# Batch 0's second halves behind all its first halves, four half transposes and two query pairs moved to DMA, and fewer bytes of loads in flight

## The chip, the cores and the metric

The kernel runs on one core of a Trainium2 chip. The metric is the device time of one execution in microseconds; the lower, the better. The core has five engines with queues of their own: TensorE (PE), which multiplies matrices; VectorE (DVE) and ScalarE (ACT), which copy and combine; GpSimd (POOL), which adds a little arithmetic and issues the loads from memory; and SyncE (SP), which issues the other transfers. The transfers themselves run on 16 shared DMA engines.

## The reference

The program is an attention with sorted blocks, followed by a bilinear feed-forward network. Four batches of eight heads, 768 positions and head width 64:

```python
for _ in range(5):                              # Sinkhorn steps on an 8x8 matrix per head
    P = np.exp(P - np.max(P, axis=-1, keepdims=True))
    P = P / (np.sum(P, axis=-1, keepdims=True) + 1e-09)
    P = P / (np.sum(P, axis=-2, keepdims=True) + 1e-09)
k_sorted = einsum('bhij,bhjcd->bhicd', P, k_blocks)      # mixes the 8 blocks of 96 rows
v_sorted = einsum('bhij,bhjcd->bhicd', P, v_blocks)
attn = softmax(scale * q_block @ k_sorted_block.T)       # within each block of 96
x = (attn @ v_sorted_block), heads side by side          # 3072 tokens x 512
out = ((x @ w_a) * (x @ w_b)) @ w_out                    # 512 -> 1536 -> 512
```

## The kernel before

**Staging.** The four batches go one after the other through two parts. The attention part works on pairs of heads (four pairs, `p` = 0 to 3, in a batch), so that two heads of 64 fill 128 partitions. It brings q into transposed form (`qT`), mixes k and v with the spread Sinkhorn matrix (`s_all`), forms scores, exponentials and the weighted sum of v, divides, and writes the result `xp` (96 rows of a block, by block, by head). `xp` is then transposed into `xT`, the tokens of a batch along the free dimension. The feed-forward part multiplies `xT` with `w_a` and `w_b`, multiplies the two results, and multiplies that with `w_out`. Batch 0 does this plainly (L836 for the first two products); batches 1 to 3 use sums of blocks in Strassen's manner for the first two products (L930), and all batches are plain at the last (L987).

**Halves.** In batch 0 each pair is cut in two halves of four blocks (`h` = 0, 1), because the plain products need only one half of the tokens at a time: `t` = 0 needs the first halves of all four pairs, `t` = 1 the second. For a half, `q_part` makes 12 transposes on PE (L555) and one copy to `qT`. `mix_half` makes 12 products for k and 12 for v (L582), each with a copy to `kT` or `vT`. `v_part` makes four transposes of `vT` on PE (L641) and a copy to `vs`. `so_part` makes eight score products (L660), an exponential on ACT (L665), eight products with `vs` (L675), a reciprocal (L681) and the division (L686), which writes `xp`. `x_part` transposes `xp` with four products on PE (L694) and copies the result to `xT`. The first pieces of the second half of a pair wait for the division of the first half of the same pair (`st["gate", p]`, L1171).

**Later batches.** `attention` handles a whole pair at once. Its q comes either by 12 PE transposes of 128 columns and a copy (`q_part`), or, where `QDMA(b, p)` holds (L262: batch 3), by `q_wide`, two loads on POOL in pieces of 64 elements, and one transposing transfer issued on SP (L707). In the second case the score products read `qT` with a stride. Their x always goes by one transposing transfer for a pair (L702). For most pairs v goes through memory and back (L628 out, L632 back), issued on SP.

**Loads.** `load` (L378) issues the loads from memory on POOL, one after the other. For each of the first 24 loads (q, k, v of batch 0 and the parts of `w_a` and `w_b`) it counts bytes backwards through the loads already issued; where the sum passes a limit (L383), the new load waits for that earlier load to have landed. Each load also waits for the seventh before it. The sum of bytes is that of the 4-byte source.

**Order.** All work is declared as pieces with dependencies, buffers and possible engines (`Plan.add`). The order in which they are issued, and the engine of those with a choice, come from the constant `ORDER`, two characters for each piece; the pieces of an engine run in that order. Into planned gaps of PE early in the kernel `_fill` puts wide products on a constant tile that nobody reads (L1222, called filler below). So a change in `ORDER` can move any piece.

Of the kernel before, what the change touches and what calls it, by code (L numbers as in the profile page):

```python
# [16 lines left out]
def _ap(t: bass.AP, extra_offset, pattern):  # L17
    return bass.AP(tensor=t.tensor, offset=t.offset + extra_offset,
                   ap=[list(p) for p in pattern])
# [17 lines left out]
class Plan:  # L37
# [192 lines left out]

RATE = 365e3
ORDER = (
    b"%z1C$e###%#'#)#+#/#-#1#5$g$i#7#;$k$m#A$o#=$q$s#G#3$u$w#C#M$y%^${#I$}#9#S%`%#%%#Y%'#O#?%)%+"
    b"#`#E%-%/#U#f%1%~%3#[#K%5#l&$%7%9#b#r%;#Q%=#W%?#x%A#h%C&@%E#n#^%G&B%I%K#t%M#d#~%O%Q%S#j$(#z"
    b"%U$.&_#p%W&a%Y$4%b%f#v%d$:%[$$&&%h&H)/&(%j&K%n%l&D&*#|%p&G&2$*&L&-&c$@&4$0%r&O&.)+$6%t&e&P"
    b"&1&g$<$&%v&R&o$B$,&j')&q$2'%$F',&T$8''&k&V'-$L$>&X&m&6&}$H)-'0&Z'#'f&8%x&^'^'h&:'b%|'j$D'a"
    b"&<'d$R$N&s'm'C&>&u'?-j'E&w'n'A'G(($J'p'J($$T'O(+$X'K(&'1'N'Q&y-r'|&|(,'3$P(#*0(/$Z*<$_*@-l"
    b"*>$V$a*2*D*B(>*8*4*F(D$]'S(@*6(J-_*H(P(F*:*T(V$c*J(L-Z(](B*V-c*P(c(R'U*L-e*](i(H*m'W(X-f*N"
    b"(N*X(_*R(T*o(o(e(0-i*u*a(u(Z-](k*Z(2({-a(a,8)%*_(q(4,:*c-v(g(6'Y(w*i(8*e(m+f'](}-p*g+i(s(:"
    b")''5*k(<*q(y)1+n'7*s'9)3)7+q)#'r)=*w';+r'=))-n-1+t't+j'v,4+l)9'x,<,7-t'z+v,>,]-3--)5,`+x,D"  # L240
    b")C,@-0,F-x*})?,C*y+z*{)I);+|+~+))O+%,H)E++)U,J,L,N)[)K+1+#)b)A+-,P+')Q)h,$)G+/,&)n)W+A+3)M"
    b")t,()^+C,*)S)z,e,,+I+5)d,g)Y*$+9)j+7,i)`**.Z+=)p,k,R.^+;)f,T+Y,V)v)l.c+?+M)|)r+[.e+O+b*&.g"
    b"+E)x,m+U/1*,.i+G/3)~,a+K,o-5,c*(+^-7+Q*..k,{-9,q,}+S.m+`,s+W-;._,.,00.+d.a/Y0*00,X/].y,2.o"
    b"0-.{,u.P,w.q-=,y,Z-?-#-A-%/^-'-C.(1E-)/`/5-+-K/7/--M.*/0/9.s.,/b.u/A.w../;-z/C/d/f.0/=/K-O"
    b"/M.}/h-Q-|/#/?.R/%-~02.T-E.$04.<-G-I06/j.&-S.V0>.>080@/E.A/O/l-U.2/G/Q.X/I.B/S-W/x0H0:/z/n"
    b".F.D/p0<0J1H/r/|/t1r/~/v.H1t.41I1v0$.J1L1z.6.L1x1M1|0B25.81~1O0D.N2$0F1U2&1Q.:1W2*2(1[1S26"
    b"202,1^221l1Y2.1`1b282:1h0L2<1j1d1n0N2>0P2B1f0V2D0X0]2@2_0c2H0_2a1q2F2Y2J2g0e0i2N0Z2c2i0o2L"
    b"2e0u0a2m2T0k2[2P2o2V0{2k0q2R2q1%0g4P0w2s4T2]2y3'0m4V2{3#2u3)0s3+4R2}2w3/1+3-4X313K0}0y4Z33"
    b"5#3M3%351'3S114]3F371-3O5%173U3;1#391=3Y3Q3A1)3=3[3C3G3W3?4e4_3j3^1/4g3`5O133z3I6L3f3h3l19"
    b"4a5Q4F151?1;3b6$4c/'0&3d4o6&3|3o5W4q/)5'5Y4H0(5)5S1A4#5[4<4J5|/+5U4L5^5d5~5+5f6(4$5-4(6*4N"  # L250
    b"5/5`4&6,4i/U4*514k574m4,5n5b4>0R594s6.4A425p/W4u534w4B0T646044664.5h55475r3p6N4D485j5t6S5l"
    b"625v6{405;6Q6}3r4:5=7#5?3t7'7%3v687)6V6T7+6:6X7>7-3x6<6_7/6Z6a73716e6]7?79756g7;6u6c776i6k"
    b"7A7C6q6>7E6s6w6m7G6@6o7K7I6y6B7M7h6D7O7c7j7Q6F7p7S7l7r7W7U7v7n7d7^7Y7x7`8*7t7[7z7|5A7f8&80"
    b"5C8(8,7~82848$5E88868.8T8:5G8<8O8V8>5I8]8@8X8_8D8B8c8Z8P8J8F8e8L8s8a8H8y8i8R8v9O8k9;4y5K8m"
    b"8x4{5M8g9'5x8o9Y4}8q6H5z8{9)8}9E6J9,9#9[9-919%9^9`9/9b9d939f9G969Q9I9l979T9h9n:u9U9j9=99:w"
    b"9r:'9K9?9p9W9t:y9A:}9x9M9v;#:{:(9z9~;'9C;79|;%;):$:*:,;-;+:.:0;:;3:4:2;/:6;5:J:8;1::;<;=:<"
    b";A;?:@:>;C:L;E:F:B;[:H;G;I:D;K:O:P;M:T:R;Q;O:V;^:X;W;S;Y:Z:o:];U:_;a;b:a;f;d:e:c;h:q;j:k:g"
    b":m;l<$;n:i;p:t<4;r;v<';t<H;|;~;x<R;z<)<J<T<L<6<W<><N<8<:<P<]<X<<<@<_<Z<B<*<b<D<c<,<F<.<0<e"
    b"<2"
)  # L260
STRASSEN_OUT = ()
QDMA = lambda b, p: b >= 3  # L262
VDMA = lambda b, p: 4 * b + p >= 6


@with_exitstack
def kernel(
# [11 lines left out]
    nc = tc.nc  # L279
    P = 128  # L280
    B, H, S, D = q.shape
# [96 lines left out]
    def load(fn, nbytes, deps=(), get=(), rank=0.0, many=0.0, spare=0.4):  # L378

        ds, way, behind = [d for d in deps if d is not None], nbytes, None  # L380
        for k in reversed(range(len(ld_n))):
            way += ld_n[k][1]
            if way > 2.8e6 and len(ld_n) < 24 and behind is None:  # L383
                behind = ld_i[k]
                ds.append(ld_n[k][0])
        if len(ld_n) >= 7:
            ds.append(ld_n[-7][0])
        i = add("POOL", 0.72 + many, fn, ds + ld_i[-1:], get=get, rank=rank, lat=0.0)
        i.behind = behind
        ld_i.append(i)  # L390
        d = add("DQ", nbytes / RATE, None, [i], rank=rank)
        ld_n.append((d, nbytes))
        return add("NIL", 0.0, None, [d], lat=spare)
# [151 lines left out]
    st = {}  # L545
# [47 lines left out]
    def mix_half(b, p, what, h, rk, after=None):  # L593
        pe = add("PE", 0.3, lambda: mix_half_pe(b, p, what, h),
                 [(k_in if what == "k" else v_in)[b, p], s_ok[b, p], after],
                 get=[("bank", (what + "m", b, p, h))], put=[(what + "2", b, p)], rank=rk)
        op = add((("ACT", 0.48), ("DVE", 0.56)), None, None,
                 [pe, o_pads, first.get((what + "T", b, p))],
                 get=[(what + "T", (what + "T", b, p))] if h == 0 else [],
                 put=[(what + "m", b, p, h)], rank=rk)  # L600
        first[what + "T", b, p] = op
        op.fn = lambda: mix_half_copy(op.eng, b, p, what, h)
        return op

    def mix_copy(eng, b, p, what, h, tc_order):
        mix, to = buf((what + "m", b, p)), buf((what + "T", b, p))
        i0, n = (0, NB) if h is None else (h * NBH, NBH)
        o0 = 0 if h is None else h * HK
        if tc_order:
            copy(ENG[eng], _ap(to, o0, [[2 * HK, P], [1, n * BLK]]),  # L610
                 _ap(mix, i0 * CG, [[1024, P], [1, n * CG], [P, NCH]]))
        else:
            copy(ENG[eng], _ap(to, o0, [[2 * HK, P], [CG, NCH], [BLK, n], [1, CG]]),
                 _ap(mix, i0 * CG, [[1024, P], [P, NCH], [CG, n], [1, CG]]))
# [86 lines left out]
    def x_dma(b, p):  # L701
        nc.sync.dma_start_transpose(  # L702
            out=_ap(buf(("xT", b)), p * S, [[KA * S, P], [BLK, NB], [1, BLK]]),
            in_=buf(("xp", b, p)).rearrange("q i e d -> q (i e d)"))

    def q_dma(b, p):
        nc.sync.dma_start_transpose(  # L707
# [56 lines left out]
    def v_part(b, p, h, vsrc, rk):  # L764

        pe = add("PE", 0.28 if h is not None else 0.5, lambda: v_pe(b, p, h), [vsrc, o_ident],
                 get=[("bank", ("vp", b, p, h))], put=[("vT", b, p)], rank=rk)
        alts = (("ACT", 0.6), ("DVE", 0.42)) if h is not None else (("ACT", 1.0), ("DVE", 0.69))
        op = add(alts, None, None, [pe, o_pads, first.get(("v", b, p))],
                 get=[("vs", ("vs", b, p))] if h in (0, None) else [],  # L770
                 put=[("vp", b, p, h)], rank=rk)
        first["v", b, p] = op
        op.fn = lambda: v_copy(op.eng, b, p, h)
        return op
# [21 lines left out]
    def x_part(b, p, h, src, rk):  # L796
        pe = add("PE", 0.2, lambda: x_pe(b, p, h), [src], get=[("bank", ("xq", b, p, h))],
                 put=[("xp", b, p)], rank=rk)
        op = add((("ACT", 0.48), ("DVE", 0.36)), None, None, [pe, x_home(b)],
                 put=[("xq", b, p, h)], rank=rk)  # L800
        op.fn = lambda: x_copy(op.eng, b, p, h)
        xT_done.setdefault((b, h), []).append(op)
# [358 lines left out]
    for p in range(HP):  # L1161
        rk = float(p)
        qd = q_part(0, p, 0, rk)
        kd = mix_half(0, p, "k", 0, rk)
        vd = v_part(0, p, 0, mix_half(0, p, "v", 0, rk + 0.05), rk + 0.1)
        m = so_part(0, p, 0, True, kd, qd, vd, rk + 0.1)
        x_part(0, p, 0, m, rk + 0.15)
        st["last", p] = m
    R0 = 10.0
    for p in range(HP):  # L1170
        st["gate", p] = st["last", p]  # L1171
    for p in range(HP):
        rk = R0 + 5.0 * p
        go = st["gate", p]
        qd = q_part(0, p, 1, rk, go)
        kd = mix_half(0, p, "k", 1, rk, go)
        vd = v_part(0, p, 1, mix_half(0, p, "v", 1, rk, go), rk + 1.0)
        m = so_part(0, p, 1, True, kd, qd, vd, rk + 1.0)
        x_part(0, p, 1, m, rk + 2.0)
    for p in range(HP):  # L1180
        load_pair(1, p, -2)
    later_spreads(5)
# [128 lines left out]
```

## Time and profile before

| | |
|---|---|
| three runs, median (lowest to highest) | 246.19 us (242.65 to 248.73) |
| the profiled execution, its own time | 246.94 us |
| its span on the core | 245.2 us |
| PE busy | 234.2 us (96%), 2180 products |
| DVE, ACT, POOL busy | 152.3, 116.0, 110.4 us |
| largest groups on PE: last products L987, 275 of them | 64.7 us, 379 ns each by their modelled ends |
| L694 transposes of x, 32 of them | start to start 0.17 to 0.26 us for four |
| transposing transfers: 12 of xT, 4 of qT | issue to landing, median 3.3 and 5.1 us |
| DMA | 27.88 MB, 114 GB/s in the mean |

The page shows one profiled execution. Products on PE are pipelined and their ends are modelled, so the busy times of single products overlap; what a group of them costs is read from its start to the start of the next group. Three runs of this kernel lie up to 6 us apart.

### The profile page before, as it was taken

The page shows a single profiled execution, that of the slowest core. Times are in us where ns is not written, and L with a number is a line of the kernel's source. Part 1 is how long each engine was busy: PE and PEld are TensorE (multiplying, and loading weights), DVE is VectorE, ACT ScalarE, POOL GpSimd, SP SyncE. Part 2 cuts the span into 40 slices and gives each one's busy share as a digit, 9 for nine tenths or more (in the row PEclk, how much of TensorE's full clock was granted, in tenths as well). Part 3 has the DMA queues.
Part 4 walks back from the last instruction along what each step waited for, and adds up shares of the span by engine and source line. Part 5 has one row for each costly group of instructions (what it writes and reads, how often), then busy time and mean ns, then how long its engine had stood idle before and what let it go on. Part 6 is the DMA issues. An engine that isn't in the chain of part 4 may idle for free.

```text
span 245.2 us, 5464 instructions
## 1 busy us (share of the span) xinstructions
PE 234.2 (96%) x2180; PEld 134.8 (55%) x2196; DVE 152.3 (62%) x305; ACT 116.0 (47%) x174; POOL 110.4 (45%) x123
## 2 busy tenths in 40 slices
PE   8698999999999999999999999999999999999992
PEld 3366856576656555565564454665654455565440
DVE  6657517886657467478884455787673458877410
ACT  3266712565447361665653541666630065563110
POOL 8789994999500000539996001373440004433000
PEclk9999569999999999999999999999999999999998
DMA  5999999999994759444999699600053352000056
GB/s 67 177 202 168 188 170 190 133 131 199 202 213 107 83 151 174 86 86 65 156 177 142 129 206 141 148 4 1 3 64 64 86 114 60 0 0 3 0 128 128
DMA packets 50104, 27.88 MB, mean 114 GB/s; under 512 B 28832, under 2 KB 47008, under 8 KB 50080
## 3 DMA queue, kind: packets, MB, share of 16 engines
q0 software_dynamic: 24112, 14.16, 42.7%
q1 hardware_dynamic: 25968, 13.38, 29.2%
q8 instruction: 17, 0.28, 0.5%
q14 instruction: 7, 0.06, 0.1%
HBM read 30.29 MB, written 8.26 MB: 157 GB/s over the span
## 4 chain that ended last, share of the span: by engine, by line
PE 81%; POOL 6%; DMA 4%; issue 3%; SPq 2%; ACT 2%; DVE 1%; ACTq 0%
PE ps L930 29%; PE ps L987 21%; PE ps L836 14%; PE ps L675 3%; PE ps L660 3%; POOL hT L373 2%; DMA q<-in_q_dram 2%; PE ps L582 2%; PE ps L571 2%; PE ps L555 2%; DMA vs<-vd 2%; PE ps L641 2%; SPq L702 1%; POOL q L434 1%; PE ps L1222 1%
## 5 line engine op out<-in xcount | busy, mean ns | idle before, releaser
L987 PE MATMUL ps<-w_out_sb,hT 128*128 128x512 bf16 x275 | 64.7, 379 | 0.9 <-issue 0.3
L373 DVE TENSOR_TENSOR f<-f,ps 128x768 f32<-128x768 f32 x54 | 49.8, 952 | 22.3 <-PE ps L930 12.2
L373 POOL TENSOR_TENSOR hT<-f 128x384 bf16<-128x384 f32 x35 | 34.4, 999 | 49.7 <-DVE f L373 49.7
L936 ACT COPY f<-ps 128x768 f32<-128x768 f32 x54 | 42.2, 800 | 30.1 <-PE ps L930 29.8
L987 PEld LDWEIGHTS <-hT 128*128 128x128 bf16 x288 | 26.8, 98 | 29.4
L665 ACT ACTIVATE eT<-ps 96x768 bf16<-96x768 f32 x32 | 25.0, 809 | 17.2 <-PE ps L660 15.4
L373 DVE TENSOR_TENSOR hT<-a,ps 128x384 bf16<-128x384 bf16 x42 | 22.0, 550 | 16.8 <-PE ps L836 12.7
L930 PE MATMUL ps<-tx,ws_a 128*128 128x384 bf16 x108 | 26.4, 326 | 0.1
L930 PE MATMUL ps<-tx,ws_b 128*128 128x384 bf16 x108 | 26.4, 326 | 0.0
L686 DVE TENSOR_TENSOR xp<-ps,rec 96x512 bf16<-96x512 f32 x32 | 21.6, 683 | 0.7
L836 PE MATMUL ps<-xT,w_a_sb 128*128 128x384 bf16 x96 | 19.5, 343 | 0.0
L836 PE MATMUL ps<-xT,w_b_sb 128*128 128x384 bf16 x96 | 19.3, 334 | 0.0
L930 PEld LDWEIGHTS <-ws_b 128*128 128x128 bf16 x144 | 14.1, 98 | 9.3
L930 PEld LDWEIGHTS <-ws_a 128*128 128x128 bf16 x144 | 13.6, 98 | 9.9 <-ACT f L936 0.5
L373 POOL TENSOR_TENSOR tx<-xT 128x768 bf16<-128x768 bf16 x2 | 3.3, 1635 | 34.5 <-DMA xT<-xp 34.5
L847 ACT CAST a<-ps 128x768 bf16<-128x768 f32 x12 | 9.3, 800 | 19.6 <-PE ps L836 19.6
L930 PE MATMUL ps<-xT,w_a_sb 128*128 128x384 bf16 x72 | 17.6, 326 | 0.0
L930 PE MATMUL ps<-xT,w_b_sb 128*128 128x384 bf16 x72 | 17.6, 326 | 0.0
L966 ACT CAST a<-ps 128x384 bf16<-128x384 f32 x18 | 8.6, 478 | 18.9 <-PE ps L930 18.9
L316 ACT CAST kT<-ps 128x768 bf16<-128x768 f32 (+1 forms) x19 | 12.9, 683 | 8.8 <-PE ps L571 6.6
L316 ACT COPY o<-ps 128x512 f32<-128x512 f32 x15 | 8.6, 589 | 17.2 <-PE ps L987 14.2
L318 DVE COPY o<-ps 128x512 f32<-128x512 f32 x9 | 6.2, 690 | 14.2 <-PE ps L987 13.8
(95 smaller groups left out, 332.0 us busy)
## 6 DMA issues: line engine op xcount, KB each, us to landing
out_dram<-o SPq DMA_DIRECT2D x48, 128.0 KB, 2.4
k<-in_k_dram POOLq DMA_DIRECT2D x16, 192.0 KB, 5.7
v<-in_v_dram POOLq DMA_DIRECT2D x16, 192.0 KB, 6.0
vd<-vm SPq DMA_DIRECT2D x10, 192.0 KB, 2.5
vs<-vd SPq DMA_DIRECT2D x10, 192.0 KB, 3.1
q<-in_q_dram POOLq DMA_DIRECT2D x16, 96.0 KB, 5.6
w_a_sb<-in_moe_w_a_dram POOLq DMA_DIRECT2D x4, 384.0 KB, 6.2
w_b_sb<-in_moe_w_b_dram POOLq DMA_DIRECT2D x4, 384.0 KB, 6.0
```

The lines of the kernel that those rows point to most:

```text
L316: nc.scalar.copy(out=out, in_=in_)
L373: ENG[eng].tensor_tensor(out=out, in0=in0, in1=in1, op=op)
L660: nc.tensor.matmul(sc[:, e, i * BLK:(i + 1) * BLK], lhsT=kT[e * D:(e + 1) * D, at:at + P], rhs=rhs, start=True, stop=True)
L665: nc.scalar.activation(out=buf(("eT", b, p, h))[:, :, 0:HB], in_=buf(("sc", b, p, h))[0:BLK, :, 0:HB], func=AF.Exp, scale=float(scale))
L675: nc.tensor.matmul(ops_[:, e, i * OW:(i + 1) * OW], lhsT=eT[:, e, i * BLK:i * BLK + P], rhs=vs[:, h * NBH + i, e * OW:(e + 1) * OW], start ...
L686: nc.vector.tensor_tensor(out=_ap(xp, h * NBH * 2 * D, [[NB * 2 * D, BLK], [D, 2], [2 * D, NBH], [1, D]]), in0=_ap(ops_, 2, [[1024, BLK], ...
L836: nc.tensor.matmul(pf[:, u, 0:HW], lhsT=w_sb[:, kc, (m + u) * P:(m + u + 1) * P], rhs=buf(("xT", b))[:, kc, t * HW:(t + 1) * HW], start=(k ...
L847: ea = add("ACT", 0.8, lambda: nc.scalar.copy(out=buf(("a", b, t, m)), in_=buf(("pf", b, t, m, "a"))[:, :, 0:HW]), [ps_["a", 1]], get=[("a ...
L930: nc.tensor.matmul(buf(key)[:, n, 0:HW], lhsT=lf(n, j), rhs=rf(j), start=start and j == 0, stop=j == 1, skip_group_check=not start)
L936: return add("ACT", 0.8, lambda: nc.scalar.copy(out=buf((name, b, g)), in_=buf(kA)[:, :, 0:HW]), [dep], get=[("f", (name, b, g))], rank=rk)
L966: e21 = add("ACT", 0.48, lambda: nc.scalar.copy(out=buf(("c21", b, g))[:, 0, :], in_=buf(kA)[:, 0, 0:HW]), [p4], get=[("a", ("c21", b, g)) ...
L987: nc.tensor.matmul(po, lhsT=hT[:, t * 2 + m // G, m % G, c * P:(c + 1) * P], rhs=w_out_sb[:, m, :], start=(m == 0), stop=(m == KO - 1), sk ...
```

## The change

The change has four parts, and a new `ORDER`.

1. The gate of the second halves of batch 0: every pair now waits for the division of the first half of pair 3, the last declared, where each waited for its own.
2. The x of the second halves of batch 0: no longer four PE transposes and a copy for each pair, but one transposing transfer of half size for each, issued on SP.
3. `QDMA` holds for pairs 2 and 3 of batch 2 also. Their q is loaded by two loads with small pieces and transposed by a transfer on SP, in place of one load, 12 PE transposes and a copy.
4. The limit on the bytes of loads on their way goes from 2.8 to 2.3 MB.

```diff
-QDMA = lambda b, p: b >= 3
+QDMA = lambda b, p: 4 * b + p >= 10
 VDMA = lambda b, p: 4 * b + p >= 6
+XDMA = lambda p: True
+WHOLE = lambda p, what: False
...
-            if way > 2.8e6 and len(ld_n) < 24 and behind is None:
+            if way > 2.3e6 and len(ld_n) < 24 and behind is None:
...
+    def mix_first(b, p, what, rk):
+
+        if not WHOLE(p, what):
+            return lambda h, r, after=None: mix_half(b, p, what, h, r, after)
...
+    def x_half_dma(b, p, h):
+        nc.sync.dma_start_transpose(
+            out=_ap(buf(("xT", b)), p * S + h * HB, [[KA * S, P], [BLK, NBH], [1, BLK]]),
+            in_=buf(("xp", b, p))[:, h * NBH:(h + 1) * NBH].rearrange("q i e d -> q (i e d)"))
...
     for p in range(HP):
-        st["gate", p] = st["last", p]
+        st["gate", p] = st["last", HP - 1]
     for p in range(HP):
         rk = R0 + 5.0 * p
         go = st["gate", p]
         qd = q_part(0, p, 1, rk, go)
-        kd = mix_half(0, p, "k", 1, rk, go)
-        vd = v_part(0, p, 1, mix_half(0, p, "v", 1, rk, go), rk + 1.0)
+        kd = st["mix", p][0](1, rk, go)
+        vd = v_part(0, p, 1, st["mix", p][1](1, rk, go), rk + 1.0)
         m = so_part(0, p, 1, True, kd, qd, vd, rk + 1.0)
-        x_part(0, p, 1, m, rk + 2.0)
+        if XDMA(p):
+            d = sp_dma(1.3, 0.65, lambda p=p: x_half_dma(0, p, 1), [m, x_home(0)],
+                       put=[("xp", 0, p)], rank=rk + 2.0)
+            xT_done.setdefault((0, 1), []).append(d)
+        else:
+            x_part(0, p, 1, m, rk + 2.0)
```

`mix_first` with `WHOLE` false is `mix_half` under another name, so the mixes themselves are unchanged. The string `ORDER` is replaced as a whole (not shown). With it the engines' orders differ from the fourth piece of attention on. On PE the first halves now come ahead of every second half: in before the second-half mixes of pair 0 stood before the v transposes of pair 3's first half; in the new kernel the first piece of a second half, q of pair 0, comes after three of the four first-half L675 groups, that of pair 3 among them. Of the 24 groups of L836 for `t` = 0, the first now comes with fewer second-half pieces ahead of it: without the k mix and q of pair 3, the v transposes of pairs 2 and 3 and two of the score groups, and with one L675 group more. The fillers become 43 products where they were 36. On POOL, two spreads of `s_all` stand together after the second pair of weight parts, and the weight sums stand at other places between the loads. On SP the four half transposes come first, and the two new q transposes stand among the transfers of v and x of batches 1 and 2.

More of the change, by code (lines that the diff above doesn't have):

```diff
@@ L232 @@
 ORDER = (
[L233 to L259, printed above, removed]
+    b"$e%z1C###%#'#)#+#/#-#1#5$g$i#7#;$k$m#A$o#=$q$s#G#3$u$w#C#M$y%^${#I$}#9#S%`%#%%#Y%'#O#?%)%+"
+    b"#`#E%-%/#U#f%1%~%3#[#K%5#l&$%7%9#b%;#Q#r%=#W%?%A#h%C&@%E#n#^#x%G&B%I%K#t%M#d%O%Q%S#j#z%U&_"
@@ new lines @@
+    b"#p#~%W&a%Y%b$(%f#v%d$.%i$$&&&D%[&(%j$4%n&F%m&*)-%p&c#|&-&2$*&g&e&.&j$0%r&4&H&1$6&k$:&J&o%t"
+    b"&n$&$<$@&L&q%v$,$B$F$2&O%x&s%}$8&P)+&u&6&R&w$>&8&}$H&:')'#)/((',&<'%(*&?'-''&T$D'0&y'G&V&{"
+    b"'1$L&X'^'I'b$N-j'3'a'K'e&Z$J'C&]'5'N'?'E'7'f'9$R'A*0'h';$T-v*<*2*4$P*8$X'=*>-r*6$Z*D*H*:$V"
+    b"*@$_*e(>$a'O*B-l'Q*J*F$]*L*P(@(D-Z'n*a-_(J'p(F*N-]$c(P-c(L*c(V-a(B*g*i(]*R(R($'|(H(c(&'S*k"
+    b"(X*m'~-p(N*T(_'U'W(,'j(T*V(/(i'Y(e'l-e*X(o(Z*]-g(k'r(u*Z-i(a'['t(0({'v*o(2(g)%(q*_'x*q*u)1"
+    b"(4(m(w*s(6)7(8,a'z)=+j*w(:,c+f(s(})C,4+l+i-t,<(y)',7+v(<,?,$+n,&,@)I+p)#)3,]+x)O,8,C))+r,_"
@@ new lines @@
+    b")U+)+u-x,:,{+z,},D)9+|+++~,F-n+5+1,H)5+9,J,L)[,N+;)?,P,(+7,*,,*y);)b+=*}+?*{)E+#+%)K,R+M)A"
+    b")h,T+')Q+-)G)n+O,V)W+/+U)M)t-1)^+3+Y-3)S,e)d)z+A,g)Y*$-5)j+C-7,i)`**/1+I)p+[,k-9)f/3+Q-;/-"
+    b"+b)l+S/0)v+E+W)r/A+G/C+^,m+K)|,q._,o,s-=/5+`)x/7.a*&/Y--,..c+d-?)~-/.Z/90.,0.^*,-A00.F.e/["
+    b"*(-C,X.g,u-#,w.y,y.H.{/;.2*.-%.K0*,2-'.L,Z-K02-M-E04.P/=.i-)0,-G-I061E-O.k.N.o-Q/b-S.q.R/?"
+    b".4/d-U.T0H-+0>.6.(0J.V080@.m/f.8/E-W.*/G/K/I.,/^0:.X-z/M../h/`.:1G1I0<.s-|1K/j/x.0-~.u.}.w"
+    b".</z.$/l/#/%/O.&.>/Q0B/S.@1M0D.B0L0F1O1Q0N/n0P1U/p1S0V1r.D1W0X0]/r1m1Y1t0c/t1[/v0_1z1^1v0e"
@@ new lines @@
+    b"0i1|1b0Z1`0o2$1x1h0u0a1d2&0k1j1~1f0{4T0q2(2*1%4V0g3'4P0w24202,0m3)22263+2.0s4R3/1n3-2:3128"
+    b"/|332</~0}0y3E0$355#2B1+1'1q372>2D3;395%1-111#2H2@3A3G3=2J1)3C2F173?135S1=2L2N5U193K2T3J1/"
+    b"4e3M5O1?2P2V2Z153O4g2R2X3S1;3Q5Q2]2_3U6$2a3k3W3Y6&1A5|2g3[2c2i3`3^5~2m2e3l3f3b2o3h2}2k3d5n"
+    b"2q5p2s3n4X6L2y5'4Z3#2u5)2{4]5+/'0&572w3p594_5-3%/U0(5A5/5W/)5C64/W5Y4(660R51/+5[4F4a0T535^"
+    b"5d6N4H4c4*4J6(556Q4-3z4L6*5`6R4.4N4i6T3|5f3r4k5b4#6,4<3t4m4$406.3v5;4>4&5=5E5?4@5h42605G5j"
+    b"4B3x5I5l625r444D5t7C5v464o7E48687G6:4q6<7K7I4s7M6V4:4u7O7c6X7Q4w6_7S6Z6a7W7U6e6]7d7^7Y6g7`"
@@ new lines @@
+    b"6u6c7[6i6k7f806q6>826s6w6m846@6o88866y6B8:7h6D8<8O7j8>6F7p8@7l7r8D8B7v7n8P8J8F7x8L8*7t8H7z"
+    b"7|6{8R8&6}7#8(8,7~7%7'8$7=7+7)8T8/7-8V8X7/8]8Z718_738s8a798c7?7;758e8y778i7A8g8v9E8o9Y8q8k"
+    b"9O4y6H8m8x5K6J914{5M5x8{4}9G8}9Q9J939#9S5z9'96979[9%9;9K9^999`9U9b9d9M9=9f9h9@9W9l9j9A9)9n"
+    b":,:'9+9r:.9C9-9p:09t:49x9/9v:6:2:(9z9~::9|:J:8:<:$:*:P:@:>:R:T:M:F:X:V:B:Z:H:o:]:D:_:O:u:a"
+    b":y:w:e:c:{:q:}:k:g;7:m;#;%:i;':t;=;);A;?;-;+;C;9;E;3;/;5;G;[;I;1;K;<;b;M;f;d;Q;O;h;^;S;W;j"
+    b";Y<$;n;U;l<*;a<4;p<>;r;v<';t<R;|;~<6<@<8<,<C;x<:<.<];z<0<)<<<T<D<_<2<V<H<X<a<F<c<J<Z<L<N<e"
@@ L260 @@
+    b"<P"
 )
 STRASSEN_OUT = ()
-QDMA = lambda b, p: b >= 3
+QDMA = lambda b, p: 4 * b + p >= 10
 VDMA = lambda b, p: 4 * b + p >= 6
+XDMA = lambda p: True
+WHOLE = lambda p, what: False
 @with_exitstack
@@ L603, in mix_half, with part @@
         return op
+    def mix_first(b, p, what, rk):
+        if not WHOLE(p, what):
+            return lambda h, r, after=None: mix_half(b, p, what, h, r, after)
+        pe = add("PE", 0.46, lambda: mix_pe(b, p, what),
+                 [(k_in if what == "k" else v_in)[b, p], s_ok[b, p]],
+                 get=[("pair", (what + "m", b, p))], put=[(what + "2", b, p)], rank=rk)
+        def part(h, r, after=None):
+            op = add((("ACT", 0.48), ("DVE", 0.56)), None, None,
+                     [pe, o_pads, first.get((what + "T", b, p))],
+                     get=[(what + "T", (what + "T", b, p))] if h == 0 else [],
+                     put=[(what + "m", b, p)], rank=r)
+            first[what + "T", b, p] = op
+            op.fn = lambda: mix_copy(op.eng, b, p, what, h, False)
+            return op
+        return part
     def mix_copy(eng, b, p, what, h, tc_order):
@@ L1163 @@
         qd = q_part(0, p, 0, rk)
-        kd = mix_half(0, p, "k", 0, rk)
-        vd = v_part(0, p, 0, mix_half(0, p, "v", 0, rk + 0.05), rk + 0.1)
+        km = mix_first(0, p, "k", rk)
+        kd = km(0, rk)
+        vm = mix_first(0, p, "v", rk + 0.05)
+        vd = v_part(0, p, 0, vm(0, rk + 0.05), rk + 0.1)
+        st["mix", p] = km, vm
         m = so_part(0, p, 0, True, kd, qd, vd, rk + 0.1)
```

## Prediction

> **What bounds the kernel now.** I read first the busy table (PE 96% of the span), then the stretches of time, then the chain of waits. The stretches (columns: window, length, busy us of PE, weight loads, DVE, ACT, POOL, granted clock, DMA share, GB/s) cut the span where its character changes:
>
> ```profile
> 14.00:24.30 10.30, 8.95 (x262) 6.97 (x257) 8.33 (x19) 7.98 (x15) 10.28 (x11) 1.00 1.27 182
> 24.30:34.80 10.50, 10.48 (x140) 7.37 (x141) 3.89 (x9) 4.74 (x8) 10.38 (x11) 0.51 1.22 184
> 34.80:240.60 205.80, 204.21 (x1700) 115.65 (x1711) 131.77 (x216) 98.18 (x141) 79.37 (x85) 1.00 0.66 106
> 240.60:245.20 4.60, 0.00 (x0) 0.00 (x0) 0.00 (x0) 0.56 (x1) 0.00 (x0) 0.75 0.51 110
> ```
>
> After 34.8 us PE is busy 204.2 of 205.8 us at full clock: there, only PE work taken out shortens the kernel, and only 1.6 us of idling is left to win. Before 14 us everything waits for the Sinkhorn steps on the 32-row p_nat; the engines' orders are the same there in both kernels. Between lies the attention of batch 0, with idle time and with 10.5 us at half clock:
>
> ```profile
> 23.15 0.27 PE ps L582 x9
> 23.42 0.89 issue
> 24.32 0.25 PE ps L582 x3
> 24.57 0.54 PE ps L641 x4
> ```
>
> This is the chain of waits (start, us, what). A group of 12 small products is cut after nine; nothing that the profile shows is waited for, and what follows runs at half clock: the four L641 transposes take 0.54 us here, 0.33 us at 15.94.
>
> **The skill.** "TensorE: Matmul & The Clock Gate", Part 1, says that the PE clock halves when its activity is low, that this is judged in free-running windows of about 3.4 us, and that it comes back after a busy window. The trace agrees in kind: clock 0.51 from 24.3 to 34.8, and the return 3.8 us after the dense L836 products began at 30.95. That the stretch of small products before, 87% busy, brought it about is my reading. Part 2 of the page says that matmuls stay in program order: a wait on one holds all behind it. "DMA: Bandwidth & Descriptors", Rules for kernel authors, says that a DMA transpose may run next to ordinary DMAs, and that all queues share the same 16 engines. The trace agrees: transposes take 2.8 us to land in quiet and up to 6.5 in busy stretches.
>
> **PE work that goes.** Timeline rows (start, us, engine, line, operands):
>
> ```profile
> 47.24 0.34 PE L694 MATMUL ps<-ident,xp 96*128 96x96 bf16 x4
> 47.42 0.81 PE L836 MATMUL ps<-xT,w_b_sb 128*128 128x384 bf16 x4
> ...
> 77.75 0.84 PE L555 MATMUL ps<-ident,q 128*64 128x128 bf16 x24
> 78.52 0.51 PE L660 MATMUL ps<-qT,kT 64*128 64x96 bf16 x16
> ```
>
> Start to next start is what counts. An x group (four L694) costs 0.18 us here; the other three cost 0.17, 0.17 and 0.26: 0.78 us for the four second halves. The q of pairs 2 and 3 of batch 2 are exactly the 24 rows at 77.75: 0.77 us. Together **-1.55 us**, all in the saturated part. Four xT copies and two qT copies (0.36 to 0.55 us each) leave ACT and DVE, which have slack there (DVE 132 of 206 us, ACT 98): nothing. The scores of those pairs read q with a stride; all 256 score products, batch 3's strided ones too, stand at 202/203/278 ns: nothing.
>
> **The wait.** Every second-half q and k/v product now waits for L686 of pair 3, first half. I walk the new order from 14.4 with durations from this trace (12 products 0.29, four vT 0.33, eight scores 0.28, eight o 0.36, exp 0.80, copies 0.42 to 0.56, 0.2 us from PE to a reader). The vT copy of pair 0 lies behind the second spread on DVE and ends at 15.86; the scores of pair 0 end at 16.6, of pair 1 at 17.5. ACT then has k copy, exp, v copy, exp: the exp of pair 3 ends at 20.4. DVE does the vs copy of pair 3 to 19.8 and the L686 of pair 0 to 20.5. The o of pair 3 stands behind the x of pair 0 on PE and ends at 21.25; DVE still has a vs copy (to 20.9) and the xT copy of pair 0 (to 21.4), then reciprocal 0.20 and L686 0.69: the gate opens at **22.35**. Held behind it on PE are q, the mixes, and in their wake everything of the second halves; ACT and DVE are then short of work. From there PE is fed, and L836 starts at about 28.0, where the row of before is 30.95, or 28.65 at full clock (next step). But less is done by then: one mix (0.29), one q (0.30), two vT (0.66) and two scores (0.56) fewer, one o (0.36) more, so 1.45 us. Net 28.0 + 1.45 - 28.65 = +0.8 us if the new kernel is spared the 0.89 us halt, +1.7 if it has one. I take **+1.3**. Bounds: -0.9 (ACT and DVE run ahead, no halt) to +3.5 (two more dependency steps of 0.9 are exposed).
>
> **The clock.** In before, 24.3 to 31.16 is 6.85 us of small products that would be 4.58 at the prices from before 24.3: 2.3 lost. From 30.95 to 34.73, 12 L836 products take 3.78 us and would take 1.95: 1.8 lost. Together 4.1 us. If the clock falls at the same place, the new kernel has some 3.7 us of small work left before L836 instead of 4.6: a loss of 1.85 + 1.8, so **-0.4**. Bounds: -4.1 (it doesn't fall) to +1.9 (it falls a window of 3.4 us earlier, in the gap at the gate, at the ratio 6.85/4.58).
>
> **x by DMA.** Four issues on SP, which has no work from 1 to 66 us. The first product of t=1 needs all four. Between the last pair's o and that product stand one L836 group and twelve groups of batch 1 (mixes, q, v, scores): 0.65 + 5.5 = 6.1 us. The chain is 0.2 + 0.2 + 0.69 and a landing of 2.8 to 6.5, median 3.3 for xT and 5.1 for qT under load: 3.9 to 7.6. With 5.1 it is 6.2, so **+0.1**; bounds 0 and +1.5. The landings, the first line for xT, the second for qT:
>
> ```profile
> DMA to landing us min/median/max: 2.8/3.3/6.4
> ...
> DMA to landing us min/median/max: 2.7/5.1/6.5
> ```
>
> **Loads.** The bound touches only the first 24 loads: counted back in bytes, w_a's first part now waits for k of pair 2 instead of v of pair 1, w_b's for k of pair 3. POOL executes in order, so two spreads (2.0 us each) and a weight sum (1.65) behind come later, and so do the weight parts behind them. By the landings of before (6.0 to 6.5 us) the second pair of parts goes from 28.0 and 30.8 to about 30.5 to 32 and 33 to 34.5, the last from 33.4 and 35.6 to about 35 to 37 and 37.6 to 39.4. Full clock needs them at 30.6, 34, 38 and 39: 0 to 1.4 us late; at half clock all in time. k of pair 2 of batch 1 issues near 40.2 instead of 36.3 and is needed from 46.5 on. I take **0**; bounds 0 and +4. Two more q halves in 256-byte pieces add two POOL issues (0.83 each) and double time on the queue, near 65 to 75 us; the transposes wait for them on SP, ahead of v and x of batch 1 and 2, which before were issued from 75 on and are needed from 83 (sums on DVE). Cover enough: 0; bound +1.5.
>
> **Sum.** -1.55 + 1.3 - 0.4 + 0.1 = -0.55 on the profiled execution's 246.94 (span 245.2 and 1.7 around it): 246.4. That execution is 0.75 above the median 246.19, so I forecast **245.6**. All other waits of the new order are taken as the old ones, 1.6 us in 206.
>
> **Rivals.**
> 1. *The clock holds.* The first halves alone leave gaps in which the new order has seven more wide filler products (43 against 36, 0.22 us each at speed); these may keep the activity up. For it: clock 1.00 until 24.3 with fillers up to 15; against: a filler at 19.6 did not prevent the fall. Time: 245.6 - 3.7 = 241.9, and 241.0 without the halt.
> 2. *Late loads bind (slower).* POOL in order behind its waits makes the weights, then k and q of pair 2 of batch 1, miss PE. With landings of 7.8 us, as q has between 60 and 80 us, and each POOL step behind its predecessor, the lag is 4; if the half clock also begins one window earlier (+1.9), 251.5. It decides once PE stands over 5.5 us at L836 or L571 between 30 and 55 us. For it: DMA share 1.2 to 1.3 up to 70 us. Against: before never waits for a weight, and late PE hides late loads.
> 3. *Nothing to be seen.* Gate and saved work cancel, both around 1.5 us, under the spread of 242.65 to 248.73: the likeliest case, with its numbers above.
>
> **Numbers.** The likeliest, with its bounds and the runs' spread: 243 to 249, chance 0.57. Rival 1, 240 to 243: 0.18. Rival 2, 249 to 254: 0.25. Faster by over 2% (under 241.3, about what a measurement of this kernel tells from no change) is the lower part of rival 1: 0.14. Slower by 2% (over 251.1) is most of rival 2: 0.22. Range 240.5 to 251.5.
>
> **What would show it.** L686 of pair 3 near 22.3 and L555 right behind; L836 from 28 (full clock) or 30.5 (half); 16 L694 and 24 L555 products fewer; PE idle after L836 still under 3 us; clock about 0.5 for some 10 us. I am wrong if PE waits for a DMA at the first product of t=1, if weights are waited for, or if the half clock lasts much longer or is absent.

## The result and the profile after

| | before | after |
|---|---|---|
| median of the runs (lowest to highest) | 245.72 us, 4 runs (242.65 to 248.73) | 254.57 us, 4 runs (252.34 to 255.62) |
| the profiled execution, and its span | 246.94, 245.2 us | 255.62, 253.9 us |

The changed kernel is **slower**: ratio 1.039, 95% interval 1.026 to 1.052. The forecast was 245.6 us in a range of 240.5 to 251.5; the result lies 3 us above that range. Medians here and below are over all executions, ratios over the fast ones alone, since single executions of a kernel come out more than 1.5% above its fastest.

The stretches of the changed kernel, in the columns of the prediction's first fence (the last column but two is the granted clock):

```profile
14.00:24.30 10.30, 9.68 (x241) 6.75 (x239) 7.38 (x18) 6.05 (x11) 7.00 (x10) 1.00 1.04 141
24.30:34.80 10.50, 8.55 (x161) 5.98 (x154) 4.23 (x10) 5.72 (x12) 9.68 (x8) 0.97 1.01 148
34.80:60.00 25.20, 22.05 (x286) 13.91 (x285) 15.84 (x32) 12.40 (x18) 21.40 (x25) 0.95 1.27 163
60.00:80.00 20.00, 17.90 (x153) 10.29 (x153) 8.31 (x16) 7.37 (x10) 13.00 (x17) 0.83 1.40 187
80.00:249.10 169.10, 168.67 (x1266) 91.30 (x1263) 105.49 (x163) 80.79 (x117) 47.27 (x50) 1.00 0.52 92
```

The same stretch from 34.8 to 80 in the kernel before:

```profile
34.80:80.00 45.20, 44.96 (x557) 28.78 (x557) 30.32 (x62) 23.70 (x33) 26.26 (x30) 1.00 1.05 168
```

Three things are to be seen. The half clock from 24.3 to 34.8 is gone (0.97 where it was 0.51). From 14 to 34.8 the loads come at 141 and 148 GB/s where they came at 182 and 184. And from 34.8 to 80 PE, which before was busy 45.0 of 45.2 us at full clock, now idles 5.25 us and has lower clocks, 0.95 and 0.83. After 80 us it is saturated again. PE's last work ends at 249.1 instead of 240.6: the 8.5 us arise before 80.

What PE waited for (line, releaser: us in total, times, longest):

```profile
PE ps L861 <- DMA xT<-xp: 4.7, 2, 3.4
PE ps L861 <- DMA w_a_sb<-in_moe_w_a_dram: 2.0, 1, 2.0
PE ps L557 <- DMA q<-in_q_dram: 1.9, 2, 1.4
```

L861 is L836 of before. Its two waits are new: before, PE waited neither for a transposed x nor for a weight. The timeline of PE around both:

```profile
33.42 0.82 PE L861 MATMUL ps<-xT,w_a_sb 128*128 128x384 bf16 x4 [1.95 <-DMA w_a_sb<-in_moe_w_a_dram]
34.08 1.42 PE L861 MATMUL ps<-xT,w_b_sb 128*128 128x384 bf16 x4
35.29 1.49 PE L861 MATMUL ps<-xT,w_a_sb 128*128 128x384 bf16 x4
36.57 1.95 PE L861 MATMUL ps<-xT,w_b_sb 128*128 128x384 bf16 x8
...
58.37 0.32 PE L861 MATMUL ps<-xT,w_a_sb 128*128 128x384 bf16 x1 [1.27 <-DMA xT<-xp]
62.10 0.48 PE L861 MATMUL ps<-xT,w_a_sb 128*128 128x384 bf16 x1 [3.41 <-DMA xT<-xp]
63.93 2.74 PE L861 MATMUL ps<-xT,w_a_sb 128*128 128x384 bf16 x8
66.92 1.47 PE L861 MATMUL ps<-xT,w_b_sb 128*128 128x384 bf16 x4
68.60 0.82 PE L861 MATMUL ps<-xT,w_b_sb 128*128 128x384 bf16 x4
```

Each wait is followed by rows at half clock: four products take 1.42 to 1.49 us instead of 0.82, and start to start 1.21 and 1.28 us instead of 0.65. The granted clock is 0.5 from 34.14 to 37.55 us and from 61.45 to 68.27. So these two waits cost themselves and then more than half as much again: 2.0 + 1.7 us at 33, and 4.7 + 3.1 us at 57 to 68. (The second terms are half of the time in which PE works at half clock, where a product takes twice its time.) Not every wait has this tail: 1.5 us of waiting for w_a in run e9 and 1.8 us for w_b in run e1 below are followed by full clock.

The chain of waits names what was late at the second place (start, us, what):

```profile
51.09 0.37 DVE xp L706
51.46 0.24 issue
51.69 0.11 DVE hT L375
51.80 10.26 DMA xT<-xp
62.06 0.04 issue
62.10 0.48 PE ps L861
```

L706 is the division. The half transpose of the last pair goes out 0.3 us after it and takes 10.26 us to land. The four half transposes alone, first and last issue, then their landings:

```profile
L727 SPq DMA_TRANSPOSE xT<-xp x4: 1180/1228/1490, 29.2 to 51.8; - x4
...
DMA to landing us min/median/max: 4.7/8.4/10.3
```

The first, at 29.20, had no other transpose near it and landed in 4.7 us; the other three went out at 46.15, 49.21 and 51.80, where POOL had k, v, q and w_out on their way, and landed in 7.8, 9.1 and 10.3 us.

### The profile page after: what moved, and what is told of

It is laid out like the page before. It is cut to its first block, busy times and chain, and to the rows that moved or that the text cites. A ratio compares the mean times of both kernels' runs of the same rounds, so it can differ in the third digit from the quotient of the medians.

```text
span 253.9 us, 5405 instructions
## 1 busy us (share of the span) xinstructions
PE 237.8 (94%) x2162; PEld 132.9 (52%) x2162; DVE 149.5 (59%) x299; ACT 117.3 (46%) x176; POOL 107.8 (42%) x123
## 4 chain that ended last, share of the span: by engine, by line
PE 73%; DMA 19%; POOL 3%; DVE 1%; issue 1%; ACT 0%; DVEq 0%; ACTq 0%; SPq 0%
PE ps L955 33%; PE ps L1012 20%; PE ps L861 13%; DMA vd<-vm 5%; DMA k<-in_k_dram 4%; DMA xT<-xp 4%; DMA w_b_sb<-in_moe_w_b_dram 3%; PE ps L680 2%; PE ps L695 2%; DMA w_a_sb<-in_moe_w_a_dram 2%; POOL s_all L524 2%; PE ps L573 1%; PE ps L639 1%; DMA vs<-vd 1%; PE ps L557 1%
## 5 line engine op out<-in xcount | busy, mean ns | idle before, releaser
L375 POOL TENSOR_TENSOR hT<-f 128x384 bf16<-128x384 f32 x37 | 36.4, 1000 | 95.6 <-DVE f L375 95.2
L1012 PE MATMUL ps<-w_out_sb,hT 128*128 128x512 bf16 x288 | 66.6, 379 | 0.0
L861 PE MATMUL ps<-xT,w_a_sb 128*128 128x384 bf16 x96 | 21.2, 353 | 6.6 <-DMA xT<-xp 4.7
L318 ACT COPY o<-ps 128x512 f32<-128x512 f32 x17 | 9.8, 587 | 29.5 <-PE ps L1012 27.2
L706 DVE TENSOR_TENSOR xp<-ps,rec 96x512 bf16<-96x512 f32 x32 | 21.8, 684 | 0.8
L861 PE MATMUL ps<-xT,w_b_sb 128*128 128x384 bf16 x96 | 20.8, 348 | 0.0
L701 DVE RECIPROCAL rec<-ps 96x8 f32<-96x8 f32 x32 | 6.2, 197 | 22.0 <-PE ps L695 21.9
L955 PE MATMUL ps<-xT,w_a_sb 128*128 128x384 bf16 x72 | 17.6, 326 | 0.0
L955 PE MATMUL ps<-xT,w_b_sb 128*128 128x384 bf16 x72 | 17.6, 326 | 0.0
L441 POOL DMA_DIRECT2D v<-in_v_dram x16 | 11.8, 734 | 7.2 <-PE ps L639 2.4
L695 PEld LDWEIGHTS <-eT 96*128 96x128 bf16 x256 | 12.0, 100 | 4.7 <-issue 0.5
```

Source lines behind the costliest of these rows:

```text
L318: nc.scalar.copy(out=out, in_=in_)
L375: ENG[eng].tensor_tensor(out=out, in0=in0, in1=in1, op=op)
L441: nc.gpsimd.dma_start(out=buf((name, b, p)), in_=_ap(t, (b * H + 2 * p) * S * D, [[W, P], [S * D, 2], [1, W]]))
L695: nc.tensor.matmul(ops_[:, e, i * OW:(i + 1) * OW], lhsT=eT[:, e, i * BLK:i * BLK + P], rhs=vs[:, h * NBH + i, e * OW:(e + 1) * OW], start ...
L701: nc.vector.reciprocal(out=buf(("rec", b, p, h)), in_=_ap(buf(("op", b, p, h)), 0, [[1024, BLK], [512 + D, 2], [OW, NBH]]))
L706: nc.vector.tensor_tensor(out=_ap(xp, h * NBH * 2 * D, [[NB * 2 * D, BLK], [D, 2], [2 * D, NBH], [1, D]]), in0=_ap(ops_, 2, [[1024, BLK], ...
```

## The experiments

Two theories stood at first. **The transposes**: those issued at 46 to 52 us do the harm, through the wait at the first product of t = 1 and the half clock after it. **The limit**: loads start late, so weights, k and q come late. A third was the gate with its new order. Letters for theories hold within one expectation only. Each run is compared with the kernel before on the same chip.

### Undoing parts of the changed kernel

e1, the limit alone; e2, x over PE alone; e3, both; e4, the own gate:

```diff
-            if way > 2.3e6 and len(ld_n) < 24 and behind is None:    # e1, e3
+            if way > 2.8e6 and len(ld_n) < 24 and behind is None:
-XDMA = lambda p: True                                                # e2, e3
+XDMA = lambda p: False
-        st["gate", p] = st["last", HP - 1]                           # e4
+        st["gate", p] = st["last", p]
```

> The changed kernel with the limit of 2.8 MB again, all else as changed. Theory A (half transposes land late under loads: 5.0 us of waiting at t=1 and some 3 us of half clock after it): 252 to 255, the wait for xT stays near 5 us. Theory B (fewer bytes in flight starve the load stream: 2.0 us waiting for w_a, half clock after it, everything loaded later): 248 to 251, no wait for w_a, DMA near 180 GB/s between 14 and 35 us where the changed kernel has 141 to 148. Theory C (the gate): 254 to 255.

> The changed kernel with x of batch 0's second halves by PE transposes and copies again. Theory A: 246 to 249, no wait at the first product of t=1 and no half clock near 60 us. Theory B: 253 to 256, as the waits for loads remain. Theory C: 254 to 256.

> Both undone: limit 2.8 MB and x on PE; the gate, the two q transposes and the order stay. If A and B together are the cause: 243 to 247, level with the kernel before. If the gate or the order costs several us: 249 or more.

> The changed kernel with each pair's own gate again, the order of the instructions unchanged. Theories A and B: 253.5 to 255.5, since the order holds the pieces where they are. Theory C (the wait on pair 3's division): 246 to 252.

| | us, median | ratio to before, 95% |
|---|---|---|
| e1 limit 2.8 MB | 251.25 | 1.020, 1.012 to 1.028 |
| e2 x on PE | 251.53 | 1.025, 1.020 to 1.030 |
| e3 both | 249.43 | 1.015, 1.008 to 1.022 |
| e4 own gate | 256.19 | 1.039, 1.031 to 1.048 |

Each of the two parts has a share, and neither is all of it: e1 lies between what its theories A and B expected, and so does e2. e3 gives the branch in which the order itself costs several us.

With the limit back (e1) the loads run at 184 GB/s again from 14 to 24.3, but at 141 from 24.3 to 34.8, and PE still waits for weights:

```profile
PE ps L861 <- DMA xT<-xp: 3.6, 2, 2.3
PE ps L861 <- DMA w_b_sb<-in_moe_w_b_dram: 1.8, 1, 1.8
```

So the late weights are not the limit's alone; the new order on POOL, with two spreads in one place, makes a weight part late at the old limit too. The clock of e1 is 0.89 between 60 and 80. With x on PE (e2) no wait for xT is left, but the early idling is larger in its profile: from 14 to 24.3 PE is busy 7.43 of 10.30 us at a clock of 0.86. PE halts there for 2.9 us in the middle of a group of mixes, and no wait is shown for it (see the end). With both undone the clock is 1.00 in all stretches from 14 us on, and 1.5% remain. The gate as a condition costs nothing that can be seen (e4, 0.7 us above what A and B expected, with 51 fillers): `ORDER` keeps the second halves where they are, whatever the gate allows.

e10 undoes q by DMA too, so that only the gate and the new order are left:

```diff
-QDMA = lambda b, p: 4 * b + p >= 10
+QDMA = lambda b, p: b >= 3
-XDMA = lambda p: True
+XDMA = lambda p: False
-            if way > 2.3e6 and len(ld_n) < 24 and behind is None:
+            if way > 2.8e6 and len(ld_n) < 24 and behind is None:
```

> Limit 2.8 MB, x and q on PE as before; what is left of the change is the gate and the new order. If the q transposes cost the 2.2 us that PE stood between 80 and 100 us: 247 to 248 (249.4 with them). If that standing belongs to the order: 249 to 250.5.

Measured: 248.44 us, ratio 1.014 (1.005 to 1.022), beside a before of 244.89. e3, which differs by the q transposes alone, has 1.015, so these cost nothing here. The 3.5 us over before are not all the order's, though. `_fill` plans its fillers anew for each variant, and in e2, e3 and e10 it puts eleven of them between the first products of the feed-forward part, where neither the kernel before nor the changed kernel has any (57 fillers in all in these three traces, 46 in the changed kernel and 37 in before, where the description of the change has 43 and 36). In e10:

```profile
28.09 1.47 PE L860 MATMUL ps<-xT,w_a_sb 128*128 128x384 bf16 x8
29.39 2.48 PE L1254 MATMUL ps<-ws_b 128*128 128x512 bf16 x11
31.71 0.81 PE L860 MATMUL ps<-xT,w_b_sb 128*128 128x384 bf16 x4
```

They take 2.3 us of PE. e1, with the same order and limit but without them, waits 2.1 us for weights between 29 and 40; e10 waits for none. So the fillers may largely have taken the place of such waits; what this order loses to late weights and what to fillers can't be told apart by these runs. A further part lies later in e10's profiled execution (247.97, the fastest of its four):

```profile
70.00:80.00 10.00, 9.59 (x131) 5.58 (x130) 5.90 (x10) 6.11 (x9) 5.45 (x8) 1.00 1.53 203
80.00:90.00 10.00, 9.14 (x98) 4.87 (x96) 5.27 (x11) 3.35 (x5) 0.00 (x0) 1.00 1.01 207
90.00:100.00 10.00, 9.85 (x102) 5.02 (x103) 4.86 (x11) 5.99 (x10) 0.00 (x0) 1.00 0.71 166
```

PE is busy 28.58 of these 30 us, where the kernel before has 29.52: batch 1's attention finishes later, and PE waits in it for divisions (0.74 us at 90.15) and copies. That is 0.9 us more, and with the 2.3 most of the 3.5.

### One part alone on the kernel before

e5, only the half transposes; e6 and e8, only the limit; e7, only q by DMA:

```diff
-        x_part(0, p, 1, m, rk + 2.0)                                 # e5
+        d = sp_dma(1.3, 0.65, lambda p=p: x_half_dma(0, p, 1), [m, x_home(0)],
+                   put=[("xp", 0, p)], rank=rk + 2.0)
+        xT_done.setdefault((0, 1), []).append(d)
-            if way > 2.8e6 and len(ld_n) < 24 and behind is None:
+            if way > 2.3e6 and len(ld_n) < 24 and behind is None:    # e6; 3.3e6 in e8
-QDMA = lambda b, p: b >= 3
+QDMA = lambda b, p: 4 * b + p >= 10                                  # e7
```

> The kernel before with its own order and limit, and only the x of batch 0's second halves by four half transposes. Theory A (they land in 8 to 10 us next to the loads): PE waits 3 to 6 us at the first product of t=1, total 248 to 253. If the four transposes are harmless in an order that wasn't made for them: 245 to 247, the saved 0.8 us among it.

> The kernel before with only the limit of 2.3 MB. Theory B: load stream under 160 GB/s between 14 and 35 us, PE waits for a weight part or for q, 248 to 251. If the limit matters only with the changed order on POOL: 245.5 to 247.

> The kernel before with only q of pairs 2 and 3 of batch 2 by DMA. If it saves its PE work alone: 245.2. If the transposes wait on SP for their loads and hold the transfers of v and x behind them (PE stood 2.2 us between 80 and 100 us in the run with limit and x undone): 246 to 249, with PE waiting there.

> The kernel before with a limit of 3.3 MB. If bytes in flight bind before too: 243 to 245. If 2.8 MB keep the DMA engines busy already: 245 to 247.

| | us, median | ratio to before, 95% |
|---|---|---|
| e5 x by DMA | 253.32 | 1.032, 1.023 to 1.041 |
| e6 limit 2.3 MB | 249.35 | 1.017, 1.009 to 1.025 |
| e7 q of two pairs by DMA | 245.36 | 1.000, 0.997 to 1.002 |
| e8 limit 3.3 MB | 245.73 | 1.003, 1.001 to 1.006 |

The kernel before, measured beside these runs, has 245.37. x by DMA alone costs 8.0 us, nearly as much as the whole change and just above the range expected; e6, e7 and e8 fell into ranges that had been named, e7 near the case in which PE work alone is saved. The waits and the chain of e5:

```profile
PE ps L840 <- DMA xT<-xp: 5.9, 2, 4.3
```

```profile
52.42 0.28 PE ps L554 x11
52.71 9.06 DMA xT<-xp
61.76 0.04 issue
61.81 2.08 PE ps L840 x6
63.89 0.44 PE ps L674 x8
```

It is the picture of the changed kernel, on the old order and the old limit: a landing of 9.06 us, 5.9 us of waiting at the first products of t = 1 (L840 here), and six products that take 2.08 us, 0.35 each, where 0.16 is the full-clock price. The limit alone costs 4.0 us (2.2 to 6.1 by its interval; 0.7 of it can be three fillers that its plan adds at 36.1), and PE waits for the same weight part as in the changed kernel:

```profile
PE ps L835 <- DMA w_a_sb<-in_moe_w_a_dram: 2.2, 1, 2.2
PE ps L659 <- issue: 1.4, 1, 1.4
```

The sum of the single costs, 8.0 + 4.0 + 0 + the 3.5 of e10, is 15.5, and the change costs 8.9. Part of the difference is the 2.3 us of fillers in e10; the rest must overlap. How they overlap is my reading and not shown: what the loads lose before 34 us makes PE late for the second halves, and PE idles for one cause where it would have idled for the next. q by DMA costs nothing and brings nothing that can be measured, though 0.77 us of PE work are gone; the interval reaches from -0.8 to +0.6 us. A higher limit brings nothing: 2.8 MB was already enough.

### Why the landings are late, and what of it costs

e9, in the changed kernel, holds w_out and every load behind it on POOL until the half transpose of pair 3 has landed:

```diff
-            P * 4 * DMODEL * 4, rank=rank))
+            P * 4 * DMODEL * 4, xT_done[0, 1], rank=rank,
+            hold=xT_done[0, 1][-1]))
...
-        i.behind = behind
+        i.behind = behind if hold is None else hold.deps[0]
```

> The changed kernel, but the three loads of w_out, and so all later loads on POOL, start only when the half transpose of pair 3 has landed. Theory A with shared DMA engines as the reason for the late landing: pair 3's transpose lands in 3 to 6 us where it took 10.3, the wait at t=1 falls from 5.0 to under 2 us, and the total to 249 to 252 unless the later loads bind. If transposes are slow there whatever else runs: landing 8 us or more, total 254 or above.

Measured: 263.64 us, ratio 1.074 (1.067 to 1.082). The last half transpose is as late as in e5:

```profile
50.77 9.07 DMA xT<-xp
59.85 0.03 issue
59.88 0.02 POOLq L465
```

The expected landing in 3 to 6 us did not come, though nothing was issued on POOL between 49.1 and 60.4. Five loads issued from 45.5 to 48.4 were still on their way. So it is not w_out alone. That one transpose holds up the next is a second possible cause: in the changed kernel the last three land at 53.9, 58.3 and 62.1 us, further apart than they were issued (46.15, 49.21, 51.80). It can't be all of it, as the first of these three, with no transpose ahead of it, took 7.8 us. No run separates the two. The wait at t = 1 does fall from 4.7 to 1.6 us, with the last landing at 59.9. The loads that were held then bound the rest, as the waits show:

```profile
PE ps L680 <- DMA qT<-q: 7.7, 1, 7.7
...
PE ps L861 <- DMA xT<-xp: 1.6, 2, 1.2
```

The last pair of runs separates the two ways in which a transpose can harm: by its own landing, or by what it does to the loads. Both leave x on PE, as in the kernel before, and add four transfers of the same 96 KB halves into a tile that nobody reads: transposes in e11, plain copies in e12.

```diff
+    def extra(b, p, h):
+        nc.sync.dma_start_transpose(                      # e11; e12: nc.sync.dma_start(out=scr[0:BLK, 0:NBH * 2 * D],
+            out=_ap(scr, p % 2 * HB, [[2 * HB, P], [BLK, NBH], [1, BLK]]),
+            in_=buf(("xp", b, p))[:, h * NBH:(h + 1) * NBH].rearrange("q i e d -> q (i e d)"))
...
-        op.fn = lambda: x_copy(op.eng, b, p, h)
+        op.fn = lambda: (x_copy(op.eng, b, p, h), h == 1 and extra(b, p, h))
```

> The kernel before, whose second halves of x still go over PE, with four half transposes of the same x added on SP into a scratch tile that nobody reads. No engine can wait for them. Theory A (the transposes harm by slowing the loads that are in flight with them): the loads issued between 44 and 58 us land in 9 to 14 us instead of 6 to 8, the data rate falls to 60 to 100 GB/s for some us, and some later work waits for a load: 247.5 to 251, while the transposes themselves land in 7 to 10 us. Theory B (the harm of x by DMA is PE's own wait for the four landings and the half clock after it): the transposes may land as late, but the time is that of before within 1.5 us (244 to 247). A third case: they land in 3 to 5 us here, because nothing of the change's other parts is there; then the lateness came from where they were issued.

> The kernel before with four plain DMA copies of the same 96 KB halves of x, SBUF to SBUF, on SP, into a scratch tile that nobody reads; bytes, moments and queue are those of the idle transposes. If it is the transposing that is slow next to loads: the copies land in 2 to 4 us, the data rate does not fall, and the time is that of before within 1 us. If it is only one more transfer in a full DMA queue: the copies land as late as the transposes, 7 to 10 us.

Measured, beside a before of 246.14: e11 245.71 us, ratio 0.995 (0.992 to 0.999); e12 245.20, ratio 0.999 (0.996 to 1.002). Four transposes that nobody waits for cost nothing. They were issued at 41.07, 47.31, 50.82 and 58.97, all beside loads, and landed in 4.6, 3.6, 8.1 and 7.4 us: the last two are late here too. Their landings together, and below them those of the loads between 44 and 64 us (KB each, median us to landing), in e11:

```profile
DMA to landing us min/median/max: 3.6/6.0/8.1
...
w_out_sb<-in_moe_w_out_dram POOLq DMA_DIRECT2D x3, 512.0 KB, 9.7
v<-in_v_dram POOLq DMA_DIRECT2D x4, 192.0 KB, 7.7
q<-in_q_dram POOLq DMA_DIRECT2D x4, 192.0 KB, 8.5
k<-in_k_dram POOLq DMA_DIRECT2D x4, 192.0 KB, 8.7
```

and the landings of the copies in e12:

```profile
DMA to landing us min/median/max: 3.9/5.0/6.2
```

The loads of the kernel before take 7.6, 6.3, 6.5 and 7.2 us for w_out, v, q and k in that stretch, those of e12 7.9, 7.0, 6.9 and 7.5. So the transposes do slow the loads, by 1.4 to 2.1 us, where plain copies add 0.3 to 0.7; but nothing waits for those loads that soon. Theory A of e11 (the harm goes through the loads) falls with the time, and its Theory B holds: the cost of x by DMA is PE's own wait for the landing, and the half clock that follows. The copies, one by one, take 4.6, 3.9, 6.2 and 5.5 us, between the two cases that were expected. So the transposing adds nothing at the first two places and 1.9 us at the last two; what else makes those two late is not shown, as no copy was measured without loads beside it. Why the changed kernel's landings reach 10.3 where these end at 8.1 stays open; more loads are on their way there at 46 to 52, and the transposes follow one another more closely.

## Why the prediction was wrong

**Right: the PE work that goes.** The 16 products of x and 24 of q are absent (16 rows of L714, 72 of the wide L557, where there were 32 and 96). Their -1.55 us stand as PE work, but half of it, the q, can't be seen in the time of e7.

**The wait: near in its dates, open in its cost.** The gate was put at 22.35 and L836 at 28.0. The q behind the gate starts at 21.92 in e1, 22.13 in e10, 23.07 in e3 and 23.56 in the changed kernel, and L861 at 27.05, 27.26, 28.59 and 28.69. The differences are not the limit's, which is 2.8 MB in the first three: the start before them moves as much. The first mix of k begins at 14.44 in before, at 15.43 in the changed kernel, and between 13.87 and 16.77 in the other runs, with either limit. What holds the second halves is the order and not the gate (e4). The cost taken was +1.3; in the 3.5 of e10 it can't be separated from late weights and fillers.

**Wrong, and the larger part: "x by DMA", +0.1 with bounds 0 and +1.5.** Its cover was worked out as 6.1 us from the last o to the first product of t = 1. The o ends at 50.76, and PE runs dry at 57.10 (58.37 less 1.27): 6.3 us. (Not the first product of t = 1 needs all four transposes, but the first four products need one each: two ran, the third and the fourth waited.) Its chain up to the issue was 1.09; it is 1.04. The step that failed is the landing: 5.1 taken, 6.5 as upper bound, 10.26 measured. Both values came from transposes issued after 76 us, when the loads of batch 0 and the weights are through; in the stretch in question no transpose of before ran, and a DMA share of 1.1 to 1.3 was in view. The "Rules for kernel authors" that the prediction drew on from the Trainium skill ("DMA: Bandwidth & Descriptors") say that a transpose may run beside ordinary DMAs; the runs agree in that it costs no time by itself (e11), and show what it does not promise, a landing time: 2.8 us in quiet, 8 to 10 here. A second term was absent: the half clock after the wait, 61.45 to 68.27. Together 4.7 + 3.1 us in the changed kernel; e5 as a whole costs 8.0.

**Wrong: "Loads", 0.** The arithmetic had two branches: 0 to 1.4 us late at full clock, in time at half clock. The trace took the first, and a little more: w_a's part was issued at 28.04 behind two spreads on POOL (3.92 us in the chain), landed at 33.37, and was needed at 31.47. I took 0 since I had the clock half at that moment. With the half clock after it, the wait costs 3.7 us; alone on the kernel before the limit costs 4.0 (e6), the upper bound. The new order has its share in it, as the 2.1 us of waiting for weights in e1 show.

**Wrong: the clock, -0.4.** The fall at 24.3 is absent (0.97), so its 4.1 us are saved, the lower bound. What brings it about isn't settled. In the new order it stays away also with the own gate, with the higher limit and with x on PE (0.98 to 1.00 from 24.3 to 34.8 in e1 to e4 and e10); all of these have fillers after 19 us, which the old order lacks and on which the rival "the clock holds" counted, and no run takes the fillers alone away. In the old order it comes and goes: 0.51 in before and e7, 0.67 in e5, 0.84 in e11, 0.91 in e12, 1.00 in e8.

What it is worth can be read from the executions of the unchanged kernel. Of the 39 measured beside e5 to e8, the 11 with a mean granted clock of 0.995 or more have a median of 244.1 us, the 23 between 0.984 and 0.995 one of 245.4, and the 5 below one of 247.5. The half clock thus goes with up to 3.4 us and with much of the spread of this kernel. The execution that the forecast was worked on had 0.974, among the lowest. A typical one has about 1.3 us to give (245.4 less 244.1), so the 4.1 separate the profiled executions and are not a gain to count on. e8 shows the same: its profiled execution, without half clock, is the fastest of its 20 (244.41), and its median is 0.4 us above that of before. In the changed kernel PE, at full clock, then ran into a weight part that was not there at 31.47. The clock and the loads were added as if independent; where weights arrive barely in time, what PE gains in reaching them it waits for them.

**The sum, redone with the trace**: -1.55 (PE work) - 4.1 (half clock of before) + 3.7 (w_a and half clock) + 7.8 (x and half clock) = +5.9 of the 8.7 between the two profiled executions. Of the remaining 2.8, 1.0 is there when the first mix of k begins (15.43 instead of 14.44, behind a wait for q), which moves from run to run. What makes up the other 1.8 is not shown; fillers and small waits of the new order are at hand.

**Of the rivals**, "the clock holds" described the clock and not the time: it did not ask what a faster PE meets. "Late loads bind" had the right side and half of the cause: its deciding point, over 5.5 us of standing at L836 or L571 between 30 and 55, was not reached (2.0 us for the weight); the rest came from the transposes, which were in no rival, though the list of signs named the wait at the first product of t = 1.

**Not found**: a version faster than the kernel before. Of the four parts only the gate (e4) and q by DMA (e7) are free, and q alone stands at before's time.

## What to carry to other kernels

The landing time of a transfer belongs to a place: take it from the stretch in which the transfer will run, and if none of its kind runs there, from the ordinary loads that do, with the whole queue ahead of it. When work leaves a saturated engine for a transfer, ask who is first to need the result and how many us before that the transfer can start; four transposes that nobody waited for were free, the same four in front of a product cost 8 us. A gain in speed and a delay of loads in the same stretch must be walked together, since the one takes away the other's cover.

## What was not expected of the hardware

- A half transpose of 96 KB, always beside loads, lands in 4.3 to 6.2 us when issued at 27 to 30 us (the changed kernel, e1, e4, e9), in 3.6 to 5.1 at 41 to 48 and 7.4 to 9.1 at 50 to 59 in the old order (e5, e11), and in 7.0 to 10.7 when issued from 43 to 52 in the new one; a plain copy of the same bytes in 3.9 to 6.2.
- After waits of 2.0 us (changed kernel) and 2.2 us (e6) PE works at half clock; after 1.5 us (e9) and 1.8 us (e1) it doesn't, and after the 0.89 us in before it does, for 10 us. The length of the wait alone does not decide. Between 14 us and PE's last work, every stretch at half clock in all fourteen traces lasts 3.41 us, or twice or three times that.
- Nearly the same order of work has the clock at 0.51 from 24.3 to 34.8 us in one execution and at 1.00 in another (e7 against e8).
- A limit of 2.3 MB of 4-byte source on the way gives 128 to 141 GB/s from 14 to 24.3 us (five traces), 2.8 MB gives 166 to 184 (eight traces); 3.3 MB gives 191 and brings no time.
- The halts of PE for which no wait is shown can last up to 2.9 us (2.9 in e2 and e12, 0.89 in before at 23.42). All nineteen of more than 0.25 us that the traces have between 14 and 32 us end 1.2 to 1.6 us after the end of a 16 KB transfer on the DMA queue that the page calls "instruction". That they are waits for PE's next instructions, late behind the loads, is my reading; no run tests it.
